# A decode-attention kernel on one core: the query product moves wholly onto VectorE, and TensorE's program begins at its second fetch block

## The chip, the cores and the metric

The kernel runs on one core of one Trainium2 chip. The metric is the time of one execution on the device, in microseconds (us). All tensors are 32-bit floats. Engines are called TensorE (PE in the profile), VectorE (DVE), ScalarE (ACT), GpSimd (POOL) and SyncE (SP). SyncE issues nearly all transfers from HBM into the on-chip memory (SBUF), in the order of its program.

## The reference

One token goes through an attention block over a cached sequence, and then through a gated feed-forward block. Both add to the token. B = S = 1, D = 640, H = 32 heads, 8192 cached positions, 192 elements per head, F = 1536.

```python
def _A_ref(x, k_cache, v_cache, wq, wo):
    q = (x @ wq).reshape(B, Sq, H, Dh) # then transposed to b h q d
    scores = jnp.einsum("bhqd,bhkd->bhqk", q, k_cache) * (Dh ** -0.5)
    p = _softmax(scores, axis=-1)
    o = jnp.einsum("bhqk,bhkd->bhqd", p, v_cache)
    return o.transpose(0, 2, 1, 3).reshape(B, Sq, H * Dh) @ wo

def _B_ref(x, W_gate, W_up, W_down):
    gate = jnp.einsum("bsd,df->bsf", x, W_gate)
    up = jnp.einsum("bsd,df->bsf", x, W_up)
    gate = gate * (gate > 0)
    return jnp.einsum("bsf,fd->bsd", gate * up, W_down)

h = x + _A_ref(_layernorm(x), k_cache, v_cache, wq, wo)
h2 = h + _B_ref(_layernorm(h), W_gate, W_up, W_down)
```

The bytes are almost all in the two caches: each head has 6144 KB of keys and 6144 KB of values, and there are 32 heads.

## The kernel before, in words

**Buffers.** Three large SBUF buffers take every big transfer in turn: `kt[0]` and `kt[1]` for the keys of even and odd heads, `vt` for the values. Before the first head they hold the query weights `wq`, which are five slabs of 128 partitions by 6144 columns: slabs 0 and 1 in `kt[0]`, slabs 2 and 3 in `kt[1]`, slab 4 in the first half of `vt`. So each buffer can be given to the cache only when its slabs have been used.

**Query product (lines 201 to 219).** The normalised token lies as five columns `xn[:, j]` over 128 partitions. For each slab j, every partition multiplies its row of 6144 weights by its own scalar and adds the row to the accumulator `qd`. The columns are split: VectorE does the first five sixths (5120, `QS` in line 201) in one instruction per slab (line 208 for slab 0, a plain product; line 211 for the others, a product and an addition in place). GpSimd does the last 1024 in two instructions per slab: a product in place in the weights' own buffer (line 213; line 209 for slab 0) and an addition (line 214). `h_q[j]` is the list of both engines' last handles for slab j. TensorE then sums `qd` over the partitions with a matrix of ones, one head at a time, into the PSUM bank `qb`: line 219 for head 0, inside its loop for the others.

**Order of the transfers.** Everything in SyncE's queue is issued strictly in order, and each issue waits in place for its buffer. The order is: the three transfers of `wq`, K of head 0 (`load_k`, line 262, into `kt[0]`, waits for `h_q[1]`), K of head 1 (into `kt[1]`, waits for `h_q[3]`), V of head 0 (`load_v`, line 265, into `vt`, waits for `h_q[4]`), K of head 2, V of head 1, and so on. From head 2 on, K waits until the reduction of the head before in the same buffer is done (line 296), and V until TensorE has used the values of the head before (line 239). These waits on two engines are written as several semaphore waits of one issue; all but the first stand in line 63.

**A head.** VectorE multiplies the keys by `qb` (line 290, 4 instructions of 128 x 3072), GpSimd folds each product's two halves together (line 292), VectorE sums over the rest (line 296), and TensorE, VectorE and ScalarE make the softmax. TensorE then multiplies probabilities and values (line 239). TensorE's part of the 32 heads is a hardware loop (line 52); `head_slot` places its first instruction at slot 88 of a block of 256 instruction slots, whatever code stands ahead of it.

**The end.** After the last head come the output projection (line 342), the second normalisation, and the feed-forward block (lines 379 and 395), whose weights are loaded into the same buffers as they come free. Ahead of the last product TensorE has an alignment instruction (line 391): it jumps to the next multiple of 256 slots.

Of the kernel before, what the change touches and what calls it, by code (L numbers as in the profile page):

```python
# [5 lines left out]
ALU = mybir.AluOpType  # L6
# [64 lines left out]
def decode_kernel(nc, x, kc, vc, wq, wo, w_gate, w_up, w_down, out):  # L71
    held = nc.snapshot_sems()
    P, Q, NQ = 128, 32, 4
    _, H, S, DH = kc.shape
# [19 lines left out]
    kf, vf = kc[0], vc[0]  # L94

    def sb(name, *shape):
        return nc.alloc_sbuf_tensor(name, list(shape), F32)[:]
# [4 lines left out]
    kt = [sb(f"kt{i}", P, TW) for i in range(2)]  # L102
    vt = sb("vt", P, TW)
    zt = sb("zt", P, DJ * F)
    qd = zt[:, 0:(H + 1) * DH]
    xrow = sb("xrow", 1, D)
    ones, ident = sb("ones", P, P), sb("ident", P, P)
# [11 lines left out]
    qb = banks[0][:, 0:DH]  # L119
# [5 lines left out]
    pe = Eng(nc, "pe", ET.PE)  # L125
    dve = Eng(nc, "dve", ET.DVE)
    act = Eng(nc, "act", ET.Activation)
    pool = Eng(nc, "pool", ET.Pool)
    sp = Eng(nc, "sp", ET.SP)

    to_pe = {n: nc.alloc_semaphore(name=f"to_pe_{n}") for n in ("mp", "m1", "exp", "ob")}
    dma_sems = {}
    landed = {}

    def load(dst, src, lane, after=(), eng=None):
        sem = dma_sems.get(lane)
        if sem is None:
            sem = dma_sems[lane] = nc.alloc_semaphore(name=f"dma_{lane}")
            landed[lane] = 0
        fn = lambda e: e.dma_start(dst, src)  # L140
        fn.dma = True
        (eng or sp).op(fn, after, sig=sem)
        landed[lane] += 16
        return (sem, landed[lane])
# [8 lines left out]
    hwq = [hw[0], hw[0], hw[1], hw[1], hw[2]]  # L153

    h_ones = dve.op(lambda e: e.memset(ones, 1.0))
# [7 lines left out]
    h_qd = pool.op(lambda e: e.memset(qd[:, H * DH:], 0.0))  # L163

    def rstd_of(dst, var, h_var, name):
        ve, sd, y, t = (sb(f"{n}{name}", P, 1) for n in ("ve", "sd", "y", "t"))
        a = dve.op(lambda e: e.tensor_scalar_add(ve, var, EPS), [h_var])
        b = act.op(lambda e: e.activation(sd, var, AF.Sqrt, bias=eps), [h_var, h_eps])
        c = dve.op(lambda e: e.reciprocal(y, sd), [b])
        d = dve.op(lambda e: e.scalar_tensor_tensor(t, y, ve, y, op0=ALU.mult, op1=ALU.mult), [a, c])  # L170
        d = dve.op(lambda e: e.tensor_scalar(t, t, -0.5, 1.5, op0=ALU.mult, op1=ALU.add), [d])
        return dve.op(lambda e: e.tensor_mul(dst, y, t), [d])
# [4 lines left out]
    for j in range(DJ):  # L177
        a = pe.op(lambda e, j=j: e.transpose(xT[:, j:j + 1], xj[:, j, :], ident[0:1, 0:1]), [hxr, h_id])
    a = dve.op(lambda e: e.reduce_sum(s1, xT, axis=AX.X), [a])
    a = pe.op(lambda e: e.matmul(pb[:, 0:1], ones, s1, start=True, stop=True), [a, h_ones])  # L180
    a = dve.op(lambda e: e.tensor_scalar_mul(mean, pb[:, 0:1], 1.0 / D), [a])
    h_xc = a = dve.op(lambda e: e.tensor_scalar(xc, xT, mean, None, op0=ALU.subtract), [a])
    a = dve.op(lambda e: e.tensor_mul(xsq, xc, xc), [a])
    a = dve.op(lambda e: e.reduce_sum(s2, xsq, axis=AX.X), [a])
    a = pe.op(lambda e: e.matmul(pb[:, 1:2], ones, s2, start=True, stop=True), [a])
    a = dve.op(lambda e: e.tensor_scalar_mul(var, pb[:, 1:2], 1.0 / D), [a])
    a = rstd_of(rstd, var, a, "x")
    h_xn = dve.op(lambda e: e.tensor_scalar_mul(xn, xc, rstd), [a])

    for k in range(2):  # L190
        a = dve.op(lambda e, k=k: e.reduce_sum(par[:, k, 0:1], ident.rearrange("p (g c) -> p g c", c=Q)[:, :, k],
                                               axis=AX.X), [h_id])
# [5 lines left out]
    h_ind = dve.op(lambda e: e.reduce_sum(ind, ident.rearrange("p (h k) -> p h k", k=NQ), axis=AX.X))  # L198
    h_ind4 = dve.op(lambda e: e.reduce_sum(ind4, ident.rearrange("p (h k) -> p k h", k=NQ), axis=AX.X))

    QS = 5 * H * DH // 6
    h_q = []
    d = q = None
    for j in range(DJ):
        w, x1 = wq_t[j], xn[:, j:j + 1]
        wd, wp, ad, ap = w[:, 0:QS], w[:, QS:], qd[:, 0:QS], qd[:, QS:H * DH]
        if j == 0:
            d = dve.op(lambda e, wd=wd, x1=x1, ad=ad: e.tensor_scalar(ad, wd, x1, None, op0=ALU.mult), [h_xn, hwq[j]])
            q = pool.op(lambda e, wp=wp, x1=x1, ap=ap: e.tensor_scalar(ap, wp, x1, None, op0=ALU.mult), [h_xn, hwq[j]])  # L209
        else:  # L210
            d = dve.op(lambda e, wd=wd, x1=x1, ad=ad: e.scalar_tensor_tensor(ad, wd, x1, ad, op0=ALU.mult, op1=ALU.add),  # L211
                       [hwq[j], d])
            t = pool.op(lambda e, wp=wp, x1=x1: e.tensor_scalar(wp, wp, x1, None, op0=ALU.mult), [hwq[j]])  # L213
            q = pool.op(lambda e, wp=wp, ap=ap: e.tensor_add(ap, ap, wp), [t, q])  # L214
        h_q.append([d, q])
    h_po = dve.op(lambda e: e.memset(po, 0.0))

    h_qb = [None] * H
    h_qb[0] = pe.op(lambda e: e.matmul(qb, ones, qd[:, 0:DH], start=True, stop=True), [h_ones] + h_q[-1] + [h_qd])  # L219

    for h in (h_po, h_par, h_id):
        pe.op(lambda e: e.nop(), [h], sig=False)
# [19 lines left out]
    for k in range(2):  # L242
        pe.op(lambda e, k=k: e.matmul(po2[:, 0:DH], par[:, k, :], ob[:, k * DH:(k + 1) * DH],  # L243
                                      start=(k == 0), stop=(k == 1)),
              takes=[(to_pe["ob"], 1)] if k == 0 else [], sig=pe.sem if k == 1 else None)
    body, pe.body = pe.body, None
    T_MAX, T_Q, T_ALL, T_V, T_O = range(5)
# [4 lines left out]
    def in_loop(h, what):  # L252
        return (pe.sem, base + 5 * h + what + 1)
# [3 lines left out]

    h_k = [None] * H
    h_kfree = [h_q[1], h_q[3]] + [None] * H
    each = lambda a: a if isinstance(a, list) else [a]  # L260

    def load_k(h):
        h_k[h] = load(kt[h % 2], kf[h].rearrange("(p r) d -> p (r d)", p=P), f"k{h % 2}", each(h_kfree[h]))

    def load_v(h):
        load(vt, vf[h].rearrange("(p r) d -> p (r d)", p=P), "v", [in_loop(h - 1, T_V)] if h else h_q[4])

    wo_v = wo.rearrange("(p j) n -> p j n", p=P)
    WJ = [0, 18, 36, OJ]
# [9 lines left out]
    for h in range(H):  # L279
        if h + 1 < H:  # L280
            load_k(h + 1)
        else:
            load_wo(0, h_kfree[H])
        load_v(h)

        k3 = kt[h % 2].rearrange("p (r d) -> p r d", d=DH)
        fold = []
        for i in range(NSUB):
            ks = k3[:, i * SUB:(i + 1) * SUB, :]
            a = dve.op(lambda e, ks=ks, h=h: e.tensor_mul(  # L290
                ks, ks, qb[:, None, :].to_broadcast([P, SUB, DH])), [h_k[h], h_qb[h]])
            fold.append(pool.op(lambda e, ks=ks: e.tensor_add(ks[:, :, 0:HD], ks[:, :, 0:HD], ks[:, :, HD:DH]), [a]))  # L292
        h_mul3[h] = a
        for i in range(NSUB):
            ks = k3[:, i * SUB:(i + 1) * SUB, :]
            a = dve.op(lambda e, ks=ks, i=i, h=h: e.reduce_sum(sc[h % 2][:, i * SUB:(i + 1) * SUB], ks[:, :, 0:HD],  # L296
                                                               axis=AX.X), [fold[i]])
# [10 lines left out]
        a = act.op(lambda e: e.mul(nb, pb[:, 0:1], -SCALE), [in_loop(h, T_ALL)])  # L308
# [15 lines left out]
    a = gather(H - 1)  # L324
    b = dve.op(lambda e: e.reciprocal(rl, oall[:, DH:DH + 1]), [a])  # L325
    for k in range(NQ):
        o_k = oall[:, k * OJ:(k + 1) * OJ]
        if k == 0:
            a = dve.op(lambda e, o_k=o_k: e.tensor_scalar(oT, o_k, ind4[:, 0:1], None, op0=ALU.mult), [a])  # L329
        else:  # L330
            a = dve.op(lambda e, o_k=o_k, k=k: e.scalar_tensor_tensor(oT, o_k, ind4[:, k:k + 1], oT, op0=ALU.mult,  # L331
                                                                      op1=ALU.add), [a])
    h_oT = dve.op(lambda e: e.tensor_scalar_mul(oT, oT, rl), [a, b])  # L333

    for g in range(NQ):
        pe.op(lambda e, g=g: e.matmul(acc[g * Q:(g + 1) * Q, :], ones[0:1, 0:Q], xrow[:, g * DG:(g + 1) * DG],
                                      start=True, stop=False), [hxr])
    h_wof = []
    for i in range(3):
        for j in range(WJ[i], WJ[i + 1], 3):  # L340
            for g in range(NQ):
                a = pe.op(lambda e, i=i, j=j, g=g: e.matmul(  # L342
                    acc3[g * Q:g * Q + 3, :], oT[:, j:j + 3],
                    wo_t[i][:, j - WJ[i]:j - WJ[i] + 3, g * DG:(g + 1) * DG],
                    start=(j == 0), stop=(j == OJ - 3)), [h_oT, h_wo[i], h_acc3])
        h_wof.append(a)
    h_w3 = act.op(lambda e: e.copy(w3, acc3), [h_wof[2]])
    for k in range(3):
        h_acc = pe.op(lambda e, k=k: e.matmul(acc, fix[:, k, :], w3[:, k * DG:(k + 1) * DG],
                                              start=False, stop=(k == 2)), [h_w3])  # L350

    h_gt = [None] * DJ
    for n, (j0, j1) in enumerate(((0, 4), (4, 5))):
        a = load(gt_t[:, j0:j1, :], rows_of(w_gate)[:, j0:j1, :], f"gt{n}", [h_wof[0]])
        h_gt[j0:j1] = [a] * (j1 - j0)
    h_dn = [None] * FJ
    for n, (j0, j1) in enumerate(((0, 6), (6, 9), (9, 10), (10, 11), (11, 12))):
        a = load(dn_t[:, j0:j1, :], rows_of(w_down)[:, j0:j1, :], f"dn{n}", [h_wof[1]])
# [6 lines left out]
    a = act.op(lambda e: e.activation(h4, acc, AF.Copy, accum_out=hs1), [h_acc])  # L365
    b = pe.op(lambda e: e.matmul(pa[:, 0:1], ones, hs1, start=True, stop=True), [a])
    c = dve.op(lambda e: e.transpose(hT, h4.rearrange("p (c j) -> p j c", c=Q)), [a])  # L367
    a = dve.op(lambda e: e.tensor_scalar_mul(hmean, pa[:, 0:1], 1.0 / (D * Q)), [b])
    h_hc = dve.op(lambda e: e.tensor_scalar(hT, hT, hmean, None, op0=ALU.subtract), [a, c])
    a = dve.op(lambda e: e.tensor_mul(hsq, hT[:, :, 0], hT[:, :, 0]), [h_hc])  # L370
    a = dve.op(lambda e: e.reduce_sum(hs2, hsq, axis=AX.X), [a])
    a = pe.op(lambda e: e.matmul(pb[:, 0:1], ones, hs2, start=True, stop=True), [a])
    a = dve.op(lambda e: e.tensor_scalar_mul(hvar, pb[:, 0:1], 1.0 / D), [a])
# [12 lines left out]
    a = project(pu, up_t, [h_up] * DJ)  # L386
    b = act.op(lambda e: e.activation(us, pu, AF.Copy, scale=hr), [a, h_hr])
    a = project(pg, gt_t, h_gt)
    a = dve.op(lambda e: e.scalar_tensor_tensor(gu, pg, 0.0, us, op0=ALU.max, op1=ALU.mult), [a, b])
    h_guT = dve.op(lambda e: e.transpose(guT, gu.rearrange("p (c j) -> p j c", c=Q)), [a])  # L390
    align = lambda e: e.addr_align(256, offset=0, max_nops=0)
    pe.op(align, sig=False)
    for j in range(FJ):
        for g in range(NQ):
            a = pe.op(lambda e, j=j, g=g: e.matmul(pd[g * Q:(g + 1) * Q, :], guT[:, j, :],  # L395
                                                   dn_t[:, j, g * DG:(g + 1) * DG],
                                                   start=(j == 0), stop=(j == FJ - 1)), [h_guT, h_dn[j]])
    o4 = sb("o4", P, DG)
    a = dve.op(lambda e: e.scalar_tensor_tensor(o4, pd, hr, h4, op0=ALU.mult, op1=ALU.add), [a])  # L399
# [39 lines left out]
```

## Time and profile before

| | |
|---|---|
| median of 3 runs | 1046.79 us (1046.3 to 1046.91) |
| the profiled execution: its own time | 1046.48 us |
| its span, from first to last instruction | 1045.0 us |
| VectorE busy | 698.4 us (67%) |
| GpSimd busy | 481.0 us (46%) |
| TensorE busy (matmul) | 342.9 us (33%) |
| ScalarE busy | 41.0 us (4%) |
| moved from HBM | 445.91 MB, 427 GB/s over the span |

The profile page shows one execution. Its second part cuts the span into 40 slices of about 26 us and gives, for each, the busy share of each engine in tenths, the clock that TensorE was granted, and the share of time in which the core's 16 DMA engines had packets in hand, with the rate. Other views answer questions about a stretch of time: the timeline lists instructions in order of start (start, duration, engine, line, operation, output<-input, count, and in brackets the idle time before and what ended it), the stages give busy times and the DMA rate between chosen times, the waits sum up who waited for whom, and the chain follows the work that ended last back to what released it. "SPq" is SyncE's queue: the start of a DMA issue there is the moment at which its waits were over.

### The profile page before, as it was taken

How to read it: one execution, taken by the hardware profiler on the slowest of the kernel's cores; microseconds unless marked ns; L12 is line 12 of the kernel's file. 1: busy time of each engine (PE TensorE's matmuls, PEld its weight loads, DVE VectorE, ACT ScalarE, POOL GpSimd, SP SyncE). 2: the span in 40 equal slices, each digit the busy share in tenths (PEclk: the TensorE clock that was granted, in tenths of full speed). 3: DMA queues.
4: the chain of work that ended last, by engine and by line, in shares of the span. 5: the costliest groups of instructions: out<-in, count | busy, mean ns of one | idle time of the engine just before them, and what ended most of it. 6: DMA issues, size and time to landing. Idle time of an engine off the chain costs nothing. (4 is left out here: it accounts for less than half of the span.)

```text
span 1045.0 us, 6621 instructions
## 1 busy us (share of the span) xinstructions
PE 342.9 (33%) x2733; PEld 127.0 (12%) x2733; DVE 698.4 (67%) x403; ACT 41.0 (4%) x138; POOL 481.0 (46%) x144
## 2 busy tenths in 40 slices
PE   0004422233333332223333333222333333322286
PEld 0001101011111110111111110111111111101123
DVE  4759877666666777766666677776666667776101
ACT  0000000000000000000000000000000000000000
POOL 3986555444445555544444555554444455555000
PEclk9999666666666665666666665656666666666688
DMA  9989999999999999999999999999999999999997
GB/s 395 442 334 425 441 429 433 436 427 431 440 427 440 429 431 435 427 438 431 429 442 427 433 435 429 438 431 431 436 429 435 433 431 438 429 433 433 433 426 330
DMA packets 11252, 446.03 MB, mean 427 GB/s; under 512 B 1253, under 2 KB 1257, under 8 KB 1898
## 3 DMA queue, kind: packets, MB, share of 16 engines
q1 hardware_dynamic: 11240, 445.91, 99.0%
q8 instruction: 4, 0.07, 0.0%
q14 instruction: 6, 0.05, 0.0%
q10 hardware_dynamic: 2, 0.00, 0.0%
HBM read 445.91 MB, written 0.00 MB: 427 GB/s over the span
## 5 line engine op out<-in xcount | busy, mean ns | idle before, releaser
L292 POOL TENSOR_TENSOR kt<-kt 128x1536 f32<-128x1536 f32 x128 | 436.5, 3444 | 466.9 <-DVE kt L290 466.9
L290 DVE TENSOR_TENSOR kt<-kt,bank 128x3072 f32<-128x3072 f32 x128 | 420.7, 3349 | 149.3 <-DMA kt<-in_A_k_cache_dram 137.0
L239 PE MATMUL bank<-vt,pr 128*2 128x384 f32 x2048 | 238.7, 635 | 544.0 <-PEq L61 544.0
L296 DVE TENSOR_REDUCE sc<-kt 128x16 f32<-128x1536 f32 x128 | 215.2, 1744 | 0.0
L239 PEld LDWEIGHTS bank<-vt,pr 128*2 128x2 f32 x2048 | 58.2, 101 | 704.2 <-issue 704.2
L302 DVE SCALAR_TENSOR_TENSOR oall<-bank,ind,oall 128x193 f32<-128x193 f32 x32 | 13.4, 420 | 138.1 <-PE bank L243 138.1
L311 ACT COPY ob<-bank 128x384 f32<-128x384 f32 x32 | 15.3, 478 | 803.3 <-PE bank L239 803.3
L243 PE MATMUL bank<-ob,par 128*128 128x192 f32 x128 | 28.4, 345 | 22.4 <-PEq L61 22.4
L243 PEld LDWEIGHTS bank<-ob,par 128*128 128x128 f32 x128 | 19.9, 189 | 44.5 <-issue 44.5
L213 POOL TENSOR_SCALAR kt<-kt,xn 128x1024 f32<-128x1024 f32 x3 | 22.6, 7536 | 0.2 <-DMA kt<-in_A_wq_dram 0.2
L233 PE MATMUL bank<-rs,ones 128*128 128x1 f32 x64 | 13.5, 280 | 27.9 <-PEq L61 27.9
L211 DVE SCALAR_TENSOR_TENSOR zt<-kt,xn,zt 128x5120 f32<-128x5120 f32 x3 | 18.1, 6041 | 5.4 <-DMA kt<-in_A_wq_dram 5.3
L219 PE MATMUL bank<-zt,ones 128*128 128x192 f32 x2 | 1.0, 593 | 57.9 <-POOL zt L214 57.9
L229 PE MATMUL bank<-zt,ones 128*128 x64 | 17.8, 361 | 0.0
L226 PE MATMUL bank<-ident,mp 128*1 128x128 f32 x32 | 8.9, 279 | 25.2 <-PEq L61 25.2
L233 PEld LDWEIGHTS bank<-rs,ones 128*128 128x128 f32 x64 | 11.7, 229 | 29.7 <-issue 29.7
L232 PE MATMUL bank<-m,ones 1*128 1x1 f32 x64 | 11.6, 248 | 9.5 <-PEq L61 9.5
L209 POOL TENSOR_SCALAR zt<-kt,xn 128x1024 f32<-128x1024 f32 x1 | 5.4, 5444 | 17.2 <-DMA kt<-in_A_wq_dram 17.2
L342 PE MATMUL bank<-kt,oT 128*3 128x480 f32 x96 | 11.5, 644 | 1.6 <-DVE oT L333 1.6
L232 PEld LDWEIGHTS bank<-m,ones 1*128 1x128 f32 x64 | 9.8, 190 | 18.3 <-issue 18.3
L367 DVE STREAM_TRANSPOSE hT<-h 128x160 f32<-128x160 f32 x1 | 0.5, 461 | 17.1 <-ACT h L365 17.1
L308 ACT ACTIVATE nb<-bank 128x1 f32<-128x1 f32 x32 | 5.5, 171 | 154.2 <-PE bank L232 154.2
(91 smaller groups left out, 125.9 us busy)
## 6 DMA issues: line engine op xcount, KB each, us to landing
kt<-in_A_k_cache_dram SPq DMA_DIRECT2D x32, 6144.0 KB, 35.5
vt<-in_A_v_cache_dram SPq DMA_DIRECT2D x32, 6144.0 KB, 21.4
kt<-in_A_wq_dram SPq DMA_DIRECT2D x2, 6144.0 KB, 24.8
kt<-in_A_wo_dram SPq DMA_DIRECT2D x2, 5760.0 KB, 34.5
vt<-in_A_wo_dram SPq DMA_DIRECT2D x1, 3840.0 KB, 14.6
zt<-in_B_W_up_dram SPq DMA_DIRECT2D x1, 3840.0 KB, 23.3
vt<-in_A_wq_dram SPq DMA_DIRECT2D x1, 3072.0 KB, 38.7
kt<-in_B_W_gate_dram SPq DMA_DIRECT2D x1, 3072.0 KB, 20.6
```

What stands on the lines that cost most here:

```text
L211: d = dve.op(lambda e, wd=wd, x1=x1, ad=ad: e.scalar_tensor_tensor(ad, wd, x1, ad, op0=ALU.mult, op1=ALU.add), [hwq[j], d])
L213: t = pool.op(lambda e, wp=wp, x1=x1: e.tensor_scalar(wp, wp, x1, None, op0=ALU.mult), [hwq[j]])
L229: return e.matmul(qb, ones, qd[:, bass.ds(i * DH + DH, DH)], start=True, stop=True)
L232: pe.op(lambda e: e.matmul(pb[:, 0:1], ones[0:1, :], m1, start=True, stop=True), takes=[(to_pe["m1"], 1)], sig=pe.sem)
L233: pe.op(lambda e: e.matmul(po2[:, DH:DH + 1], ones, rs, start=True, stop=True), takes=[(to_pe["exp"], 1)])
L239: pe.op(lambda e, i=i, g=g: e.matmul(po[g * Q:g * Q + 2, :], pr[:, 2 * i:2 * i + 2], vt[:, 2 * i * DH:2 * (i + 1) * DH], start=(i < NQ), s ...
L243: pe.op(lambda e, k=k: e.matmul(po2[:, 0:DH], par[:, k, :], ob[:, k * DH:(k + 1) * DH], start=(k == 0), stop=(k == 1)), takes=[(to_pe["ob" ...
L290: a = dve.op(lambda e, ks=ks, h=h: e.tensor_mul(ks, ks, qb[:, None, :].to_broadcast([P, SUB, DH])), [h_k[h], h_qb[h]])
L292: fold.append(pool.op(lambda e, ks=ks: e.tensor_add(ks[:, :, 0:HD], ks[:, :, 0:HD], ks[:, :, HD:DH]), [a]))
L296: a = dve.op(lambda e, ks=ks, i=i, h=h: e.reduce_sum(sc[h % 2][:, i * SUB:(i + 1) * SUB], ks[:, :, 0:HD], axis=AX.X), [fold[i]])
L302: return dve.op(lambda e: e.scalar_tensor_tensor(oall, po2, ind[:, h:h + 1], oall, op0=ALU.mult, op1=ALU.add), [in_loop(h, T_O), (dve.sem, ...
L311: act.op(lambda e: e.copy(ob, po), [in_loop(h, T_V)], sig=to_pe["ob"])
```

## The change

VectorE forms the whole row of 6144 columns for each slab, in one instruction per slab; GpSimd's nine instructions of this stage are gone, and so is the split `QS`. `h_q[j]` is now one handle, VectorE's, and the transfers and TensorE's first `qb` product wait for that one alone. The order of all transfers stays as it was. Besides, the first instruction in TensorE's list is now an alignment with `max_nops=0`, which is a jump to the start of the next block of 256 slots.

```diff
+    align = lambda e: e.addr_align(256, offset=0, max_nops=0)
+    pe.op(align, sig=False)
+
...
-    QS = 5 * H * DH // 6
     h_q = []
-    d = q = None
+    a, acc_q = h_xn, qd[:, 0:H * DH]
     for j in range(DJ):
         w, x1 = wq_t[j], xn[:, j:j + 1]
-        wd, wp, ad, ap = w[:, 0:QS], w[:, QS:], qd[:, 0:QS], qd[:, QS:H * DH]
         if j == 0:
-            d = dve.op(lambda e, wd=wd, x1=x1, ad=ad: e.tensor_scalar(ad, wd, x1, None, op0=ALU.mult), [h_xn, hwq[j]])
-            q = pool.op(lambda e, wp=wp, x1=x1, ap=ap: e.tensor_scalar(ap, wp, x1, None, op0=ALU.mult), [h_xn, hwq[j]])
+            a = dve.op(lambda e, w=w, x1=x1: e.tensor_scalar(acc_q, w, x1, None, op0=ALU.mult), [a, hwq[j]])
         else:
-            d = dve.op(lambda e, wd=wd, x1=x1, ad=ad: e.scalar_tensor_tensor(ad, wd, x1, ad, op0=ALU.mult, op1=ALU.add),
-                       [hwq[j], d])
-            t = pool.op(lambda e, wp=wp, x1=x1: e.tensor_scalar(wp, wp, x1, None, op0=ALU.mult), [hwq[j]])
-            q = pool.op(lambda e, wp=wp, ap=ap: e.tensor_add(ap, ap, wp), [t, q])
-        h_q.append([d, q])
+            a = dve.op(lambda e, w=w, x1=x1: e.scalar_tensor_tensor(acc_q, w, x1, acc_q, op0=ALU.mult, op1=ALU.add),
+                       [a, hwq[j]])
+        h_q.append(a)
...
-    h_qb[0] = pe.op(lambda e: e.matmul(qb, ones, qd[:, 0:DH], start=True, stop=True), [h_ones] + h_q[-1] + [h_qd])
+    h_qb[0] = pe.op(lambda e: e.matmul(qb, ones, qd[:, 0:DH], start=True, stop=True), [h_ones, h_q[-1], h_qd])
...
-    each = lambda a: a if isinstance(a, list) else [a]
...
-    align = lambda e: e.addr_align(256, offset=0, max_nops=0)
     pe.op(align, sig=False)
```

More of the change, by code (lines that the diff above doesn't have):

```diff
@@ L259, in decode_kernel @@
     h_kfree = [h_q[1], h_q[3]] + [None] * H
-    each = lambda a: a if isinstance(a, list) else [a]
     def load_k(h):
-        h_k[h] = load(kt[h % 2], kf[h].rearrange("(p r) d -> p (r d)", p=P), f"k{h % 2}", each(h_kfree[h]))
+        h_k[h] = load(kt[h % 2], kf[h].rearrange("(p r) d -> p (r d)", p=P), f"k{h % 2}", [h_kfree[h]])
     def load_v(h):
-        load(vt, vf[h].rearrange("(p r) d -> p (r d)", p=P), "v", [in_loop(h - 1, T_V)] if h else h_q[4])
+        load(vt, vf[h].rearrange("(p r) d -> p (r d)", p=P), "v", [in_loop(h - 1, T_V) if h else h_q[4]])
     wo_v = wo.rearrange("(p j) n -> p j n", p=P)
```

## The prediction

> **What bounds the kernel now.** I read the page first, its slices and its DMA queues, then the stages of the span, then the chain that ended last, then SyncE's queue.
>
> ```profile
> span 1045.0 us, 6621 instructions
> DMA  9989999999999999999999999999999999999997
> GB/s 395 442 334 425 441 429 433 436 427 431 440 427 440 429 431 435 427 438 431 429 442 427 433 435 429 438 431 431 436 429 435 433 431 438 429 433 433 433 426 330
> ```
>
> The transfers run at about 433 GB/s in nearly every slice of 26 us. Three slices are lower: the first (start), the last (the final products), and the third, 52 to 78 us, with 334 GB/s. The stages take that third slice apart:
>
> ```profile
> 30.00:33.00 3.00, 0.00 (x0) 0.00 (x0) 0.00 (x0) 0.00 (x0) 2.80 (x2) 1.00 0.78 336
> 46.00:63.00 17.00, 0.01 (x1) 0.04 (x1) 6.85 (x2) 0.00 (x0) 16.68 (x5) 1.00 0.70 283
> 53.00:58.50 5.50, 0.00 (x0) 0.00 (x0) 0.00 (x0) 0.00 (x0) 5.42 (x3) 1.00 0.00 0
> 58.50:59.00 0.50, 0.00 (x0) 0.00 (x0) 0.00 (x0) 0.00 (x0) 0.50 (x1) 1.00 3.89 1180
> 600.00:990.00 390.00, 121.79 (x975) 44.38 (x975) 267.99 (x143) 14.16 (x52) 177.31 (x52) 0.63 1.00 433
> ```
>
> The columns are the stretch, its length, busy time and count for PE, PEld, DVE, ACT and POOL, the clock, the DMA share and GB/s. Through 390 us of heads the DMA engines are full (1.00) while VectorE is busy for 267.99 us: the transfers bound the heads, no engine does. From 53.0 to 58.5 us nothing moves at all. The end is bound by transfers too, as the chain shows:
>
> ```profile
> 1015.26 22.25 DMA kt<-in_B_W_down_dram
> 1037.51 0.14 issue
> 1037.64 5.24 PE bank L395 x96
> ```
>
> So bytes that could have moved in that hole would bring every later transfer forward, the last one included. Why it is empty is in SyncE's queue and on GpSimd:
>
> ```profile
> 0.72 0.87 SPq L140 DMA_DIRECT2D kt<-in_A_wq_dram  x2
> ...
> 32.98 0.33 SPq L140 DMA_DIRECT2D kt<-in_A_k_cache_dram  x1
> 57.68 0.33 SPq L140 DMA_DIRECT2D kt<-in_A_k_cache_dram  x1
> 62.92 0.33 SPq L140 DMA_DIRECT2D vt<-in_A_v_cache_dram  x1
> 83.89 0.33 SPq L140 DMA_DIRECT2D kt<-in_A_k_cache_dram  x1
> ...
> SPq L63 <- POOL zt L214: 60.0, 3, 30.8
> ```
>
> K of head 0 was issued at 32.98, K of head 1 at 57.68 and V of head 0 at 62.92; the waits name GpSimd's addition (L214) for all three. K of head 0 lies in this row of the transfers (the last figure is us from issue to landing):
>
> ```profile
> kt<-in_A_k_cache_dram SPq DMA_DIRECT2D x1, 6144.0 KB, 19.3
> ```
>
> It landed at 32.98 + 19.3 = 52.3, and the next was issued 5.4 us later. The queue had simply run empty.
>
> **The query product, step by step.** The timeline of both engines:
>
> ```profile
> 18.55 2.89 DVE L208 TENSOR_SCALAR zt<-kt,xn 128x5120 f32<-128x5120 f32 x1 [10.19 <-DMA kt<-in_A_wq_dram]
> ...
> 33.05 5.55 DVE L211 SCALAR_TENSOR_TENSOR zt<-kt,xn,zt 128x5120 f32<-128x5120 f32 x1 [5.30 <-DMA kt<-in_A_wq_dram]
> 38.64 6.29 DVE L211 SCALAR_TENSOR_TENSOR zt<-kt,xn,zt 128x5120 f32<-128x5120 f32 x1
> 45.03 7.44 DVE L211 SCALAR_TENSOR_TENSOR zt<-vt,xn,zt 128x5120 f32<-128x5120 f32 x1
> 47.11 8.07 POOL L213 TENSOR_SCALAR kt<-kt,xn 128x1024 f32<-128x1024 f32 x1
> 55.27 2.34 POOL L214 TENSOR_TENSOR zt<-zt,kt 128x1024 f32<-128x1024 f32 x1
> 57.58 2.84 POOL L213 TENSOR_SCALAR vt<-vt,xn 128x1024 f32<-128x1024 f32 x1
> 60.51 2.34 POOL L214 TENSOR_TENSOR zt<-zt,vt 128x1024 f32<-128x1024 f32 x1
> ```
>
> VectorE is done with slab 3 at 38.64 + 6.29 = 44.93 and with slab 4 at 52.47; GpSimd ends slab 3 at 57.61 and slab 4 at 62.85. Its product takes 2.84 us when VectorE has stopped and 8.07 us beside it, so GpSimd, with a sixth of the columns, is the later one by ten microseconds.
>
> Price of VectorE's longer rows: 6144 columns are 1.2 times 5120. Slab 0: 2.89 x 1.2 = 3.5 us. The others: the quickest row, 5.55 us, gives 6.7 us; the slowest, 7.44, gives 8.9. With GpSimd empty in this stage the rows cannot be held up by it, so I take 6.7 and keep 8.9 as the upper bound. A second measure agrees with the lower end: the product over keys,
>
> ```profile
> L290 DVE TENSOR_TENSOR kt<-kt,bank 128x3072 f32<-128x3072 f32 x128 | 420.7, 3349 | 149.3 <-DMA kt<-in_A_k_cache_dram 137.0
> ```
>
> takes 3349 ns for 3072 columns, thus 6.7 us for 6144.
>
> Slab 0 then runs from 18.55 to 22.0 and slab 1 to 28.7: K of head 0 is issued at about 28.7 in place of 32.98. Slabs 2 and 3 cannot begin before their weights land at 33.05; they end at 39.7 and 46.4. K of head 1 is issued at 46.4 in place of 57.68. Slab 4 ends at 53.1, and V of head 0 is issued there in place of 62.92. TensorE's first `qb` product follows at once.
>
> Does that close the hole? The bytes of `wq` and of K of head 0 keep the queue busy until about 52.7, the middle between the landing at 52.3 and the last record before 53.0. From an issue to its first bytes the row at 58.50 shows 0.8 us after 57.68. So K of head 1 must be issued by 51.9; it comes 5.5 us before that. At the dear price of 8.9 it comes at 33.05 + 17.8 = 50.9, still in time. The price of the rows thus drops out of the sum. The earlier K of head 0 gains little by itself, since slab 4's weights were still in the queue at 32.98; only the 0.78 share of 30 to 33 us could hold something, at most 0.22 x 3 = 0.7 us, and I count zero.
>
> What is late next: V of head 0, 53.1 against the end of K of head 1. One 6144 KB transfer is 6.29 MB, at 433 GB/s 14.5 us, so K of head 1 ends near 67.2 and V of head 0 near 81.7. K of head 2 waits for VectorE's work on head 0. Before, that took from the first key product to the issue:
>
> ```profile
> 62.99 0.98 PE L219 MATMUL bank<-zt,ones 128*128 128x192 f32 x2 [57.86 <-POOL zt L214]
> 64.08 3.35 DVE L290 TENSOR_TENSOR kt<-kt,bank 128x3072 f32<-128x3072 f32 x1 [11.14 <-PE bank L219]
> ```
>
> 83.89 - 64.08 = 19.8 us. Now the first key product starts when `qb` is there (53.1 + 1.1 = 54.2) or when K of head 0 has landed. With transfers queued behind it, it may land late: slabs 0 to 3, issued from 0.72 on, would by bytes be in at 0.72 + 0.8 + 2 x 14.5 = 30.5 and were in at 33.05, 2.5 later, so I put K of head 0 at up to 52.7 + 2.5 = 55.2; K of head 2 is issued near 74 to 75, some 7 us before V of head 0 ends. From there on the order is the old one, shifted, and it kept the DMA share at 1.00.
>
> What was removed from GpSimd and what was added to VectorE elsewhere cost nothing: GpSimd's next work is the first fold, after the first key product, and VectorE would otherwise wait for `wq` or `qb`. The dropped second waits are those of GpSimd itself.
>
> **The jump.** No row shows an alignment at the start of a program. TensorE's first work waits for a transfer:
>
> ```profile
> 2.06 0.73 PE L178 MATMUL bank<-ident,xrow 1*128 1x1 f32 x5 [2.06 <-DMA xrow<-in_A_x_dram]
> ```
>
> A jump that takes under 2 us vanishes there, and a later TensorE delays only `xn`, behind which VectorE sits idle for 10.19 us before slab 0 (row at 18.55). So its cost at the start is zero unless it passes some ten microseconds; below zero it can't be, since nothing waits for it. The loop head keeps slot 88, so the slots of all code behind are the same. What may move is when code is fetched:
>
> ```profile
> q8 instruction: 4, 0.07, 0.0%
> ...
> q8 instruction: 1, 0.02, 1.2%
> ...
> q8 instruction: 1, 0.02, 12.8%
> ```
>
> Queue q8 fetched four blocks in the whole span, one of them at 64 to 69 us as TensorE entered its loop (second row) and the other three in the end stage, the last at 1036.0 to 1036.5 (third row). I expect the first to move to the start, and the other three to stay.
>
> **Sum.** Between 46 and 63 us the transfers moved 283 GB/s instead of 433: 17 x (433 - 283) / 433 = 5.9 us lost. The bare empty stretch gives 5.5; from the landing at 52.3 to 58.5 it is 6.2. I take 5.9. The profiled execution took 1046.48 us (span 1045.0 and 1.48 around it), which is 0.31 under the median; 1046.48 - 5.9 = 1040.6, and against the median 1046.79 - 5.9 = 1040.9. I give 1040.9.
>
> **Rivals.** (1) The gain doesn't arrive, and the time stays within 0.2% (about 2.1 us, what a measurement of this kernel can tell from no change): the kernel is bound by HBM, so moving arithmetic between engines is hidden. For it speaks the share of 1.00 over 390 us, against it the 5.5 us at zero. [...] Chance 3%.
>
> (2) The jump shifts code fetching, and the three fetches of the end stage stand before work on the chain. The most that one can cost is bounded by the last: the row of guT's transpose and the first product after it,
>
> ```profile
> 1035.23 0.84 DVE L390 STREAM_TRANSPOSE guT<-gu 128x384 f32<-128x384 f32 x1
> 1037.61 4.85 PEld L395 LDWEIGHTS bank<-kt,guT 128*32 128x32 f32 x96 [3.81 <-issue]
> ```
>
> leave 1037.61 - 1036.07 = 1.5 us. Three would be 4.6, and with the hole closed 1046.8 - 5.9 + 4.6 = 1045.5: no change that can be told. Against it: the slots are the same. [...] Chance 3%.
>
> (3) Slower: VectorE's in-place rows are much dearer at 6144 columns than the rows say, and it becomes the later engine. Its place is slabs 2 and 3, which alone stand between 33.05 and the issue of K of head 1. The gain shrinks from (51.9 - 33.05) / 2 = 9.4 us a row, is gone at (57.68 - 33.05) / 2 = 12.3, and the kernel is slower by over 0.2% from 13.4. At twice the slowest row seen, 14.9 us, the issue would come at 62.9 and the time be 1046.8 + 5.2 = 1052.0. For it speaks only the spread from 5.55 to 7.44; against it, 13.4 is 1.5 times the upper bound. Chance 2% for slower, and 2% for a row between 9.4 and 12.3, with part of the gain.
>
> **How the numbers follow.** The forecast has 90%; rivals (1) and (2) 3% each, (3) 2% and 2%. Faster 0.93, same 0.05, slower 0.02. The range takes at its low end the 6.2 us hole, the 0.7 us of 30 to 33 us and the lowest run 0.5 under the median: 1046.3 - 6.9 = 1039.4, which I cut to 1039.6; at its high end the 5.5 us hole and one exposed fetch: 1046.8 - 5.5 + 1.5 = 1042.8.
>
> **What would show it.** Right: VectorE's five rows of 3.5 and about 6.7 us; no GpSimd instruction between 1.5 and 55 us; K of head 1 issued near 46.4 and V of head 0 near 53; no zero between 46 and 63 us in the stages, with some 430 GB/s there; the first row for K waiting for its transfer and not for `qb`; the last landing near 1031.6; and the same 5 to 6 us from there to the end. Wrong: a hole anywhere before 100 us, a DMA share under 1.00 in the heads, rows above 9 us, or TensorE idle ahead of its end products for no transfer.

## The result, and the profile after

The changed kernel takes 1041.0 us (median of 5 runs, 1040.92 to 1041.24) beside 1046.79 us for the kernel before (1046.17 to 1047.87). The ratio is 0.9945, with a 95% interval of 0.993 to 0.9959. That is 5.8 us less; the forecast was 1040.9 us. The profiled execution of the changed kernel took 1040.92 us, with a span of 1039.4.

The slices of the page, to be laid beside those of before:

```profile
span 1039.4 us, 6609 instructions
DMA  9999999999999999999999999999999999999997
GB/s 396 445 429 426 441 429 431 435 433 431 433 437 430 431 438 433 426 437 431 433 431 435 433 429 437 435 426 437 429 433 431 437 433 431 435 433 432 427 425 328
```

The third slice, which had 334 GB/s, now has 429. The first and the last are nearly as they were (396 and 328, before 395 and 330). The stages that showed the hole:

```profile
30.00:33.00 3.00, 0.00 (x0) 0.00 (x0) 0.00 (x0) 0.00 (x0) 0.00 (x0) 1.00 0.80 344
46.00:63.00 17.00, 1.01 (x2) 0.50 (x2) 15.50 (x6) 0.00 (x0) 4.60 (x2) 1.00 1.03 445
53.00:58.50 5.50, 1.01 (x2) 0.50 (x2) 4.04 (x4) 0.00 (x0) 0.10 (x1) 1.00 0.99 429
600.00:990.00 390.00, 127.51 (x999) 45.66 (x1003) 261.81 (x142) 14.17 (x52) 174.60 (x52) 0.62 1.00 433
```

Between 46 and 63 us the rate went from 283 to 445 GB/s, and from 53.0 to 58.5 us from nothing to 429. (A share of 1.03 is more than there can be, so the figures of so short a stretch are good to some 3%, which is half a microsecond in 17.) The stretch of 390 us in the heads has the same 433 GB/s. SyncE's queue and VectorE, from the timeline (K of head 0, K of head 1, V of head 0, K of head 2; then, below the dots, the query product, the first key product and the first fold):

```profile
28.71 0.33 SPq L143 DMA_DIRECT2D kt<-in_A_k_cache_dram  x1
46.49 0.33 SPq L143 DMA_DIRECT2D kt<-in_A_k_cache_dram  x1
53.15 0.33 SPq L143 DMA_DIRECT2D vt<-in_A_v_cache_dram  x1
74.78 0.33 SPq L143 DMA_DIRECT2D kt<-in_A_k_cache_dram  x1
...
18.61 3.42 DVE L209 TENSOR_SCALAR zt<-kt,xn 128x6144 f32<-128x6144 f32 x1 [9.99 <-DMA kt<-in_A_wq_dram]
22.07 6.62 DVE L211 SCALAR_TENSOR_TENSOR zt<-kt,xn,zt 128x6144 f32<-128x6144 f32 x1
33.19 13.27 DVE L211 SCALAR_TENSOR_TENSOR zt<-kt,xn,zt 128x6144 f32<-128x6144 f32 x2 [4.51 <-DMA kt<-in_A_wq_dram]
46.50 6.62 DVE L211 SCALAR_TENSOR_TENSOR zt<-vt,xn,zt 128x6144 f32<-128x6144 f32 x1
...
54.96 13.15 DVE L287 TENSOR_TENSOR kt<-kt,bank 128x3072 f32<-128x3072 f32 x4 [1.39 <-DMA kt<-in_A_k_cache_dram]
58.40 13.62 POOL L289 TENSOR_TENSOR kt<-kt 128x1536 f32<-128x1536 f32 x4 [56.90 <-DVE kt L287]
```

K of head 1 is issued at 46.49 instead of 57.68. The bracket at 54.96 shows that the first key product now waits for its keys, where before it waited 11.14 us for `qb`. The chain at the end begins with the same links, earlier:

```profile
1009.00 22.94 DMA kt<-in_B_W_down_dram
1031.93 0.14 issue
1032.07 4.53 PE bank L391 x88
```

The landing that releases the last 96 products is that of the first of five loads of these weights. It came at 1037.51 before and comes at 1031.93 now, 5.58 us earlier; from there to the end of the span it was 7.49 us and is 7.47. So the gain arises before that landing, and nothing of it is lost or won behind it.

### The profile page after: what moved, and what is told of

It is laid out like the page before. It is cut to its first block, busy times and chain, and to the rows that moved or that the text cites. A ratio compares the mean times of both kernels' runs of the same rounds, so it can differ in the third digit from the quotient of the medians.

```text
span 1039.4 us, 6609 instructions
## 1 busy us (share of the span) xinstructions
PE 339.9 (33%) x2733; PEld 125.0 (12%) x2733; DVE 699.8 (67%) x403; ACT 41.1 (4%) x138; POOL 437.4 (42%) x135
## 5 line engine op out<-in xcount | busy, mean ns | idle before, releaser
L237 PE MATMUL bank<-vt,pr 128*2 128x384 f32 x2048 | 236.3, 630 | 551.1 <-PEq L61 551.1
L211 DVE SCALAR_TENSOR_TENSOR zt<-kt,xn,zt 128x6144 f32<-128x6144 f32 x3 | 19.9, 6618 | 4.6 <-DMA kt<-in_A_wq_dram 4.5
L306 ACT ACTIVATE pr<-sc,nb 128x64 f32<-128x64 f32 x32 | 11.1, 348 | 1.2 <-ACT nb L305 0.2
L227 PEld LDWEIGHTS bank<-zt,ones 128*128 128x128 f32 x64 | 9.9, 196 | 3.2
```

Source lines behind the costliest of these rows:

```text
L211: a = dve.op(lambda e, w=w, x1=x1: e.scalar_tensor_tensor(acc_q, w, x1, acc_q, op0=ALU.mult, op1=ALU.add), [a, hwq[j]])
L227: return e.matmul(qb, ones, qd[:, bass.ds(i * DH + DH, DH)], start=True, stop=True)
L237: pe.op(lambda e, i=i, g=g: e.matmul(po[g * Q:g * Q + 2, :], pr[:, 2 * i:2 * i + 2], vt[:, 2 * i * DH:2 * (i + 1) * DH], start=(i < NQ), s ...
```

## The experiments

The theory: the time follows the stretch in which no transfer is in the queue, and that stretch is set by the issue of K of head 1 alone. The rivals: the jump gives part of it; the earlier issue of K of head 0 gives part of it; the gain comes from a freed GpSimd or fewer instructions; any delay in this stage reaches the end.

**The change without its jump.**

```diff
-    pe.op(align, sig=False)   # the one at the start
```

> The changed kernel without TensorE's jump at the start. Theory (the hole in the transfers between 53.0 and 58.5 us was the whole gain, the jump is nothing): 1041.0 us within 0.5, K of head 1 issued at 46.8, no empty stretch, TensorE's first product back at about 2.06 us in place of 2.35 if the jump caused that, a code fetch at the loop's entry again. Rival (the jump gave part of the gain, by what it does to code fetching): between 1042 and 1046.8.

Measured: 1040.95 us (1040.68 to 1041.45), ratio to the kernel before 0.9944 (0.9931 to 0.9958). K of head 1 was issued at 46.63. The code-fetch queue in the stretch 0 to 2 us of the changed kernel, and in 58 to 60 us of the kernel without the jump:

```profile
q8 instruction: 1, 0.02, 3.0%
```

```profile
q8 instruction: 1, 0.02, 3.3%
```

The jump moves one code fetch of four from the loop's entry to the start of the program; the other three stay in the end stage. TensorE's first product began at 2.13 us here, at 2.35 in the changed kernel and at 2.06 before, each time on the arrival of `xrow`. The later kernels that have the jump began it between 2.06 and 2.18 us, so the 2.35 is not put down to the jump.

**The jump alone, on the kernel before.**

```diff
+    align = lambda e: e.addr_align(256, offset=0, max_nops=0)
+    pe.op(align, sig=False)
```

> The kernel before with the jump alone added at the start of TensorE's program. Theory: 1046.8 us within 0.7, the hole from 53.0 to 58.5 us still there. Rival (the jump counts): as much below 1046.8 as the kernel without the jump lies above 1041.0.

Measured: 1047.03 us (1046.55 to 1048.23), ratio 1.0002 (0.9993 to 1.0011). The stage from 46 to 63 us has its hole:

```profile
46.00:63.00 17.00, 0.00 (x0) 0.00 (x0) 6.98 (x2) 0.00 (x0) 16.81 (x5) 1.00 0.68 272
```

TensorE's first product began at 2.18 us. The two runs agree: the jump has no effect on the time that can be measured, and the whole gain is the query product's.

**VectorE alone for slabs 0 and 1 only.** For slabs 2 to 4 VectorE takes 5120 columns and GpSimd 1024, as before; GpSimd's products also wait for VectorE's row of slab 1 (`h_full`), which is done before the weights of slab 2 have landed.

```diff
+        n = H * DH if j < 2 else QS
...
+        if j >= 2:
+            t = pool.op(lambda e, wp=wp, x1=x1: e.tensor_scalar(wp, wp, x1, None, op0=ALU.mult), [hwq[j], h_full])
+            q = pool.op(lambda e, wp=wp, ap=ap: e.tensor_add(ap, ap, wp), [t, q])
```

> VectorE alone for slabs 0 and 1; slabs 2 to 4 split with GpSimd as before. This brings K of head 0 forward to about 28.7 us, and leaves K of head 1 to GpSimd's end of slab 3. Theory (only the issue of K of head 1 counts): GpSimd again ends slab 3 at about 57.6, the hole stays, 1046.8 us, at most 0.7 less. Rival (the earlier issue of K of head 0, 4.3 us, is worth something in itself): 1042.5 to 1045.

Measured: 1046.72 us (1046.59 to 1048.15), ratio 1.0001 (0.9992 to 1.001). SyncE's queue, and the stage:

```profile
28.68 0.33 SPq L143 DMA_DIRECT2D kt<-in_A_k_cache_dram  x1
57.74 0.33 SPq L143 DMA_DIRECT2D kt<-in_A_k_cache_dram  x1
...
46.00:63.00 17.00, 0.00 (x0) 0.00 (x0) 6.89 (x2) 0.00 (x0) 16.73 (x5) 1.00 0.71 289
```

K of head 0 was issued 4.3 us earlier than before, as in the changed kernel, and it was worth nothing: slab 4 was still in the queue ahead of it (in the kernel before it was issued at about 1.6 us, with 38.7 us to its landing). Three of the nine GpSimd instructions were gone here as well.

**GpSimd's part halved.** In the kernel before:

```diff
-    QS = 5 * H * DH // 6
+    QS = 11 * H * DH // 12
```

> The kernel before with GpSimd's part halved, 512 columns in place of 1024 (VectorE 5632). In the profile before, GpSimd's instructions in this stage end 2.7 us (products) or 2.2 us (additions) after a row of VectorE ends, whatever time they began: 41.32 after 38.60, 47.13 after 44.93, 55.18 after 52.47. Theory A (GpSimd waits out VectorE's whole row and only the rest scales with its columns): slab 3 ends at 55 to 56, K of head 1 is issued then, 3.5 us or so are lost, about 1044.5 us. Theory B (GpSimd runs slowly beside VectorE, in proportion to its columns): its 24.5 us for slabs 2 and 3 become 12.3, K of head 1 is issued at about 46.5, no hole, 1041.0 us.

Measured: 1044.67 us (1044.17 to 1046.23), ratio 0.9981 (0.9972 to 0.999): theory A. From its timeline:

```profile
45.82 6.90 DVE L211 SCALAR_TENSOR_TENSOR zt<-vt,xn,zt 128x5632 f32<-128x5632 f32 x1
46.82 7.33 POOL L213 TENSOR_SCALAR kt<-kt,xn 128x512 f32<-128x512 f32 x1
...
54.23 1.26 POOL L214 TENSOR_TENSOR zt<-zt,kt 128x512 f32<-128x512 f32 x1
55.47 1.56 POOL L213 TENSOR_SCALAR vt<-vt,xn 128x512 f32<-128x512 f32 x1
...
55.56 0.33 SPq L140 DMA_DIRECT2D kt<-in_A_k_cache_dram  x1
```

The product of 512 columns takes 1.56 us once VectorE has stopped, and 7.33 us when it begins beside a row of VectorE: it ends at 54.15, which is 1.43 us after that row ends at 52.72. So GpSimd's time beside VectorE was not in proportion to its columns (8.07 us for 1024 in the kernel before, 7.33 for 512): the product ended as if it had waited for the row. Half the work brings K of head 1 forward by 2.1 us only, and the time falls by 2.1.

**K of head 1 held back to slab 4.** In the changed kernel:

```diff
-    h_kfree = [h_q[1], h_q[3]] + [None] * H
+    h_kfree = [h_q[1], h_q[4]] + [None] * H
```

> The changed kernel, but K of head 1 waits for slab 4 (53.1 us) instead of slab 3 (46.5). Theory (every microsecond that the queue stands empty is a microsecond of the end): K of head 0's bytes last until 52.7, first bytes of the next 0.8 after its issue at 53.15, so 1.2 us are lost: 1042.2 us, 1041.8 to 1042.8. Rival (a short hole is made up by the transfers behind it): 1041.0.

Measured: 1042.32 us (1041.96 to 1042.68), ratio to the kernel before 0.9957 (0.9944 to 0.9971).

```profile
53.41 0.33 SPq L143 DMA_DIRECT2D kt<-in_A_k_cache_dram  x1
...
46.00:63.00 17.00, 1.01 (x2) 0.50 (x2) 15.49 (x6) 0.00 (x0) 4.32 (x2) 1.00 0.99 411
```

A hole of little over a microsecond already shows in the time, 1.3 us over the changed kernel. The transfers behind it don't make it up.

**K of head 1 held back further.** In the changed kernel, one more VectorE product:

```diff
+    h_d = dve.op(lambda e: e.tensor_scalar(vt[:, H * DH:], acc_q, x1, None, op0=ALU.mult), [a])
...
-    h_kfree = [h_q[1], h_q[3]] + [None] * H
+    h_kfree = [h_q[1], h_d] + [None] * H
...
-[in_loop(h - 1, T_V) if h else h_q[4]]
+[in_loop(h - 1, T_V) if h else h_d]
```

> The changed kernel with one more VectorE product of 6144 columns after slab 4, into the unused half of the value buffer; K of head 1 and V of head 0 wait for it. It computes nothing that is used. Issue of K of head 1 at 53.15 + 3.45 = 56.6. Theory: 56.6 + 0.8 - 52.7 = 4.7 us lost, 1045.7 us, 1045.2 to 1046.3. Rival (the gain came from fewer instructions or a free GpSimd, not from the issue): 1041.0 to 1042.

Measured: 1045.6 us (1045.32 to 1045.82), ratio to the kernel before 0.9989 (0.998 to 0.9998).

```profile
56.86 0.33 SPq L143 DMA_DIRECT2D kt<-in_A_k_cache_dram  x1
...
46.00:63.00 17.00, 1.01 (x2) 0.50 (x2) 16.85 (x6) 0.00 (x0) 2.38 (x1) 1.00 0.77 312
```

GpSimd has no part in the query product here, and VectorE has its full rows, yet 4.6 of the 5.8 us are gone again.

**The same extra product, with V of head 0 alone waiting for it.** K of head 1 waits for slab 3, as in the changed kernel.

```diff
+    h_d = dve.op(lambda e: e.tensor_scalar(vt[:, H * DH:], acc_q, x1, None, op0=ALU.mult), [a])
...
-[in_loop(h - 1, T_V) if h else h_q[4]]
+[in_loop(h - 1, T_V) if h else h_d]
```

> The same additional VectorE product, with only V of head 0 waiting for it; K of head 1 is issued after slab 3 as in the changed kernel. V of head 0 goes out at 56.6 in place of 53.15, and the first key product begins at about 56.6. Theory: K of head 1 occupies the transfers until about 67, so nothing is lost: 1041.0 us within 0.5. Rival (any delay of this stage reaches the end, through VectorE or V): 1042.6 to 1044.5.

Measured: 1040.89 us (1040.79 to 1041.09), ratio 0.9944 (0.9931 to 0.9958).

```profile
56.51 0.33 SPq L143 DMA_DIRECT2D vt<-in_A_v_cache_dram  x1
...
46.00:63.00 17.00, 1.01 (x2) 0.50 (x2) 16.85 (x6) 0.00 (x0) 2.73 (x1) 1.00 1.03 445
```

V of head 0 was issued 3.4 us later, and VectorE's busy time in this stage is that of the run before (16.85 us). The time is that of the changed kernel. Together the last two runs part the delay of VectorE and of V, which costs nothing, from the delay of the issue of K of head 1, which costs the 4.7 us between them.

**Another place: the last load cut.** In the changed kernel:

```diff
-    for n, (j0, j1) in enumerate(((0, 6), (6, 9), (9, 10), (10, 11), (11, 12))):
+    for n, (j0, j1) in enumerate(((0, 2), (2, 4), (4, 6), (6, 9), (9, 10), (10, 11), (11, 12))):
```

> The changed kernel with the first load of the down-projection weights (6 of 12 row groups in one transfer) cut into three of 2. In the changed kernel the last 96 products begin when that transfer lands and take 5.2 us. If its bytes land in order, the first products start as soon as their operand is ready, about 1.5 us earlier, and the time is 1039.7 to 1040.5. If all parts land together, as the fixed rate and the order of engines allow, it is 1041.0, or a little more for two further issues.

Measured: 1041.23 us (1040.98 to 1041.49), ratio to the kernel before 0.9948 (0.9934 to 0.9961): not faster than the changed kernel. The last products in its timeline:

```profile
1030.68 1.29 PE L391 MATMUL bank<-kt,guT 128*32 128x160 f32 x32 [1.63 <-DVE guT L387]
1032.23 0.75 PE L391 MATMUL bank<-kt,guT 128*32 128x160 f32 x16 [0.26 <-DMA kt<-in_B_W_down_dram]
1034.57 1.29 PE L391 MATMUL bank<-kt,guT 128*32 128x160 f32 x32 [1.58 <-DMA kt<-in_B_W_down_dram]
1036.13 0.48 PE L391 MATMUL bank<-kt,guT 128*32 128x160 f32 x8 [0.27 <-DMA kt<-in_B_W_down_dram]
1036.91 0.48 PE L391 MATMUL bank<-kt,guT 128*32 128x160 f32 x8 [0.30 <-DMA kt<-in_B_W_down_dram]
```

The first products did start 1.4 us earlier, as the first branch expected, but the brackets show that the later ones wait for their own loads, the last of them until about 1036.9. The second branch had the time right, but not the reason: the parts did not land together, since 32 products began at 1030.68 and the next 16 waited for their load until 1032.23. In the changed kernel, too, loading the last weights into TensorE (PEld) waited for a transfer, 0.35 us until 1036.63:

```profile
1036.63 0.16 PEld L391 LDWEIGHTS bank<-kt,guT 128*32 128x32 f32 x8 [0.35 <-DMA kt<-in_B_W_down_dram]
```

The transfers run out at nearly the same time in both kernels; this is the stretch from 1035 to 1036 us, first of the changed kernel and then of this one:

```profile
1035.00:1036.00 1.00, 1.00 (x36) 0.98 (x32) 0.00 (x0) 0.00 (x0) 0.00 (x0) 1.00 0.10 38
```

```profile
1035.00:1036.00 1.00, 0.86 (x28) 0.47 (x16) 0.00 (x0) 0.00 (x0) 0.00 (x0) 1.00 0.16 61
```

In the changed kernel TensorE is busy for the whole microsecond while the last bytes land; here it waits for them. The early start gained nothing, and no kernel tried here is measurably faster than the changed one.

## Why the prediction was right, point by point

**The hole was the gain.** The kernels of this study differ in when K of head 1 is issued, and their times follow. The prediction put the point from which a delay costs at 51.9 us; from there each microsecond should be one microsecond over the measured 1041.0.

| kernel | K of head 1 issued, us | 1041.0 + (issue - 51.9) | measured median, us |
|---|---|---|---|
| V of head 0 held back | 46.40 | 1041.0 | 1040.89 |
| changed | 46.49 | 1041.0 | 1041.0 |
| changed, no jump | 46.63 | 1041.0 | 1040.95 |
| held to slab 4 | 53.41 | 1042.5 | 1042.32 |
| GpSimd halved | 55.56 | 1044.7 | 1044.67 |
| held to the extra product | 56.86 | 1046.0 | 1045.6 |
| before | 57.68 | 1046.8 | 1046.79 |
| slabs 0 and 1 only | 57.74 | 1046.8 | 1046.72 |
| jump alone | 57.81 | 1046.9 | 1047.03 |

In the first three the issue comes ahead of 51.9 and costs nothing, so they stand at 1041.0. Eight kernels besides the one that set the base lie within 0.4 us of the line, whichever engine caused the delay. The issue times are those of one profiled execution of each kernel, the times are medians.

**The steps.** VectorE's rows cost 3.42 and 6.62 us (3.5 and 6.7 were worked out from the rows of 5120 columns). The issues came at 28.71, 46.49 and 53.15 (28.7, 46.4 and 53.1). K of head 0 landed late enough to hold the first key product until 54.96 (up to 55.2 was allowed for), and K of head 2 went out at 74.78 (74 to 75). The landing that the chain names came at 1031.93 (1031.6), and the tail behind it was unchanged. Two of the prediction's words about it are wrong: it is not the last landing, since the last of the five loads, issued at 1011.17, landed 25.4 us later, at about 1036.6; and from it to the end of the span it is 7.47 us, as it was 7.49 before, while the "5 to 6 us" fit the products alone (5.24 before). K of head 0 came earlier, and the share of 30 to 33 us hardly changed (0.78 to 0.80), so counting zero for it was right.

**The size.** The sum of 5.9 us measured 5.8 between the medians, but 5.56 between the two profiled executions (1046.48 and 1040.92), and the landing moved by 5.58. That is nearer to the bare empty stretch of 5.5, which the prediction gave beside it, than to the 5.9 that it took from the rate of a stretch of 17 us. The mechanism was right; that the forecast of 1040.9 came within 0.1 us of the median is partly luck. The chances are also added up wrongly: rivals (1) and (2), which leave the time unchanged, make 0.06 and not 0.05, and faster is then 0.92.

**The rivals.** That HBM hides the edit failed at the one place where HBM had nothing to do (0 GB/s from 53.0 to 58.5 us in the kernel before). The code fetch moved as expected and cost nothing that can be measured (1041.0 us with the jump, 1040.95 without). VectorE's rows were not dear at 6144 columns (6.62 us). That VectorE or V of head 0 is the next wait was excluded with V held back by 3.4 us (1040.89 us).

**Why GpSimd was late.** The prediction used only that its instructions were long beside VectorE. In the profile before, its products and additions were:

```profile
33.12 8.20 POOL L213 TENSOR_SCALAR kt<-kt,xn 128x1024 f32<-128x1024 f32 x1 [0.24 <-DMA kt<-in_A_wq_dram]
41.40 5.73 POOL L214 TENSOR_TENSOR zt<-zt,kt 128x1024 f32<-128x1024 f32 x1
47.11 8.07 POOL L213 TENSOR_SCALAR kt<-kt,xn 128x1024 f32<-128x1024 f32 x1
```

They end at 41.32, 47.13 and 55.18. VectorE's rows end at 38.60, 44.93 and 52.47, which is 2.7, 2.2 and 2.7 us earlier: about what the instructions take alone (2.84 and 2.34). So they end as if each had waited for the whole row and then run. With half the columns the product ended 1.43 us after its row, where it takes 1.56 alone, so only what was left after the row scaled. In the other direction the rows are mixed. VectorE's row at 45.03 lasted 7.44 us, and 47.13, when GpSimd's addition ended, to 52.47 is 5.3 of them, close to the quickest row's 5.55, as if it had waited for the addition. But the row at 38.64 lasted only 6.29 us, 0.74 more than the quickest, although GpSimd's product did not end until 41.32: had it waited for the whole of that product, it would have ended near 46.9 (41.32 + 5.55) and not at 44.93. So the times don't show one rule for both directions, and why the two engines slowed each other was not tried. What the change removed was thus a helper whose products for slabs 2 and 3 took 8.20 and 8.07 us, against 2.84 alone, so that the smaller part of the work ended last.

## What to carry to other kernels

Where transfers bound a kernel, look for the one slice in which their rate drops, and ask which issue was late and who released its buffer. Here each microsecond of an empty queue was worth one, within 0.4 us for the eight kernels beside the base, and an issue that came 4.3 us earlier onto a full queue was worth nothing (1046.72 us beside 1046.8 for the kernel before). A helper engine made this elementwise stage later: its product took 8.07 us beside a row of the main engine and 2.84 alone. Compare its durations alone and beside the other engine before splitting. A delay cost only from the point at which the queue ran dry (issues of K of head 1 up to 46.63 us cost nothing, the one at 53.41 cost 1.3 us), and that point could be worked out beforehand, from the landing of the transfer ahead.

## What the runs showed that had not been expected

Cutting the last weight load let TensorE begin 1.4 us earlier without any gain, because the last single-row loads then held the last products until 1036.91. In the changed kernel the last products began at 1036.63, and the loading of their weights into TensorE had waited 0.35 us for a transfer there too. So the end stage is held by the products and by the last loads at nearly the same time, though the chain of the changed kernel names only the first load, and easing the start alone showed nothing. What sets the time of the last loads was not tried.
